# Spectral block with a Mish MLP: order of the normalisation, banks of the first two items, place of the last deviations, order of the last contraction

## The chip, the cores and the metric

The kernel runs on one core of a Trainium2 chip. The metric is the device time of one execution in microseconds (us). A core has five engines with queues of their own, each of which works through its instructions in order: TensorE (PE in the profile; its weight loads are PEld), VectorE (DVE), ScalarE (ACT), GpSimd (POOL) and SyncE (SP), which here issues the transfers. They wait for one another through semaphores. Matmuls write into PSUM, of which the kernel uses eight banks of 128 x 512 fp32 numbers; ScalarE and VectorE read them, GpSimd does not.

## What is computed

One block with two residual branches over x (1 x 2048 x 512, fp32). Six modulation vectors come from c.

```python
mod = (_silu(c) @ w_mod).reshape(c.shape[0], 6, 1, -1)
sa, ca, ga, sb, cb, gb = (mod[:, i] for i in range(6))
h = _layernorm(x, axis=-1) * (1 + ca) + sa
x = x + ga * irfft2(rfft2(h) * (w_r + 1j * w_i))
h = _layernorm(x, axis=-1) * (1 + cb) + sb
h = einsum("bsd,df->bsf", h, w1) + b1
act = h * tanh(softplus(h))
x = x + gb * einsum("bsf,fd->bsd", act, w2)
```

The change touches the second branch (the layer norm, the MLP with Mish, 512 -> 1376 -> 512) and its borders.

## The kernel before

The 2048 rows are held as 16 tiles x[:, n, :] of 128 rows. The first branch is a DFT written as matmuls, in three phases. Its last phase runs over the 16 tiles: p3_col(n) multiplies into a bank "A" and ScalarE copies it out, p3_row(n) multiplies into a bank "B" and VectorE adds it to x[:, n, :] (line 650). norm_sums(n) (lines 109 to 112) then takes the mean and variance of the row on VectorE, and norm_scale(lo, hi) (lines 126 to 130) turns the variances of a few tiles into reciprocal deviations: Ln and Exp on ScalarE (norm_guess, lines 116 and 117), then four small operations on VectorE. Between these steps the loop at line 870 prepares w1 and the first w2 pieces: load_w2 is a transfer, gate_w2 multiplies by gb on GpSimd, sum_w2 makes four differences in tsum on GpSimd, split_w2 casts on ScalarE and subtracts on VectorE. All large products are done in fp32r with a high part and a low part (three products).

The second branch goes through 8 blocks of two row tiles (256 rows). Each block has 6 items t = 0 to 5 of the hidden layer: t = 0 is the piece of 96 columns left over, the others are two pieces of 128. So there are 48 items, numbered g = 6 b + t. For an item:

- up(g), line 719: 12 or 24 matmuls of w1 with the normalised block, into one of two banks "A". It needs an empty bank.
- mish(g), line 729: ScalarE's Mish out of that bank (line 735; this empties the bank), four additions and subtractions on VectorE (line 748) that build the seven operands of a seven-product scheme, and casts to the high part `ah` on ScalarE (line 754). `ah` has two buffers, so the cast waits until down(g - 2) has read the old one.
- low(parts), line 758: the low part `al` on VectorE (line 760).
- down(g), line 762: 21 matmuls (6 for t = 0) into the six banks of the block, two "C", two "B", two "D". It runs two items behind up (LAG = 2). RAW and SUM (lines 24 and 25) give the order of the seven groups of three matmuls: the first of RAW goes to bank 0, the next two to the halves of banks 1 and 2, then SUM to banks 3, 4, 5 and the other half of bank 1.

After the last down of a block, in item t = 1 of the next, gather copies banks 0, 4, 5 and 3 out into two buffers `h` on ScalarE (line 790), residual adds banks 2 and 1 to the two rows on VectorE (line 801), and spread does the remaining additions on GpSimd (chain, lines 795 and 796, and the four functions of rows_of, lines 807 to 810). Then store issues two transfers.

The next block's input is made in between. norm_pair(n) (line 606) normalises two tiles on ScalarE (line 140, one activation for each), into the same two buffers `h`; transpose_in (line 609) turns half of them by four matmuls (line 616) into a bank "A"; split_in (line 619) scales, shifts and splits them on ScalarE and VectorE (lines 624 to 629). norm_pair is issued in item t = 3, the transposes ahead of up in t = 4 and t = 5.

The order within each engine is the order in which the program issues its instructions (manual_schedule): mlp(s), lines 826 to 844, is one item, and the lines 899 to 924 lead from the spectral branch into the items and to finish (line 846), which does the last block's sums, on VectorE but for the function `own`, and stores its rows one after the other.

Of the kernel before, what the change touches and what calls it, by code (L numbers as in the profile page):

```python
# [15 lines left out]
N2 = 16  # L16
# [3 lines left out]
NT = 6  # L20
# [2 lines left out]
TERMS = ((0, 0), (0, 1), (1, 0))  # L23
RAW = ((0, None, 0, 0), (1, 0, 2, 1), (2, 0, 1, 6))
SUM = ((3, None, 3, 3), (4, None, 4, 4), (5, None, 5, 5), (1, 1, 6, 2))
LAG = 2


@with_exitstack
def tile_spectral_block(ctx: ExitStack, tc: tile.TileContext, x_d, w1_d, b1_d, w2_d,  # L30
                        c_d, xt_d, wm_d, wq_d, wz_d, kr_d, km_d, kc_d, ki_d, kf_d, kv_d, kw_d, kp_d, out_d):
    nc = tc.nc
# [16 lines left out]
    def bank(tag):  # L49
        return psum.tile([P, 512], F32, name="bank", tag=tag)  # L50

    def buf(tag, dt=F32):
        return work.tile([P, 512], dt, name="buf", tag=tag)
# [60 lines left out]
    def norm_guess(lo, hi):  # L114
        r = rstd[:, lo:hi]
        nc.scalar.activation(r, mv[:, lo:hi, 1], AF.Ln, bias=eps)
        nc.scalar.activation(r, r, AF.Exp, scale=-0.5)

    def norm_refine(lo, hi, sign):
        r = rstd[:, lo:hi]  # L120
        t = small.tile([P, 4], F32, name="ve")[:, 0:hi - lo]
        for out, a, one, op in ((t, mv[:, lo:hi, 1], EPS, ALU.add), (t, t, -0.5 * sign, ALU.mult),
                                (r, t, 1.5 * sign, ALU.add)):
            nc.vector.scalar_tensor_tensor(out, a, one, r, op0=op, op1=ALU.mult)  # L124

    def norm_scale(lo, hi):
        norm_guess(lo, hi)
        norm_refine(lo, hi, 1)
        nc.vector.scalar_tensor_tensor(nmr[:, lo:hi], mv[:, lo:hi, 0], -1.0, rstd[:, lo:hi],
                                       op0=ALU.mult, op1=ALU.mult)  # L130
# [6 lines left out]
    def norm(n, late=False):  # L137
        h = buf("h")
        if late:
            nc.scalar.activation(h, x[:, n, :], AF.Identity, scale=rstd[:, n:n + 1], bias=nmr[:, n:n + 1])  # L140
            return h
        nc.gpsimd.tensor_scalar(h, x[:, n, :], rstd[:, n:n + 1], nmr[:, n:n + 1],
                                op0=ALU.mult, op1=ALU.add)
        return h
# [461 lines left out]
    def norm_pair(n):  # L606
        st["h2", n] = norm(n, True), norm(n + 1, True)
# [84 lines left out]
    def split_w2(t, sums):  # L692
        hi, lo = w2[t]
        if t == 0:
            split(hi[:96], lo[:96], st.pop(("w2", 0))[0])
            return
        h, l = (w.rearrange("p e d -> p (e d)") for w in (hi, lo))
        if sums:
            split(h[:, 768:], l[:, 768:], tsum.rearrange("p e d -> p (e d)"))
        else:  # L700
            u, v = st["w2", t]
            split(h[:, 0:256], l[:, 0:256], u[:, 0:256])
            split(h[:, 256:768], l[:, 256:768], v)
# [12 lines left out]
    ups, acts, out_ps, done = {}, {}, {}, {}  # L716
    tsum = modr[:, 0:2].rearrange("p r (e d) -> p (r e) d", d=256)

    def up(g):
        b, t = divmod(g, NT)  # L720
        ups[g] = ps = bank("A")
        hh, hl = h2[b]
        parts = [(w, h, k) for w, h in ((w1h, hh), (w1l, hh), (w1h, hl)) for k in range(4)]
        for e, f, rows in tiles(t):
            for i, (w, h, k) in enumerate(parts):
                nc.tensor.matmul(ps[:rows, 256 * e:256 * e + 256], w[:, k, f * P:f * P + rows], h[:, k, :],  # L726
                                 start=(i == 0), stop=(i == 11))

    def mish(g):
        b, t = divmod(g, NT)  # L730
        ps = ups.pop(g)
        w = buf("g1")
        for e, f, rows in reversed(tiles(t)):
            c = slice(256 * e, 256 * e + 256)
            nc.scalar.activation(w[:rows, c], ps[:rows, c], AF.Mish, bias=b1n[:rows, f:f + 1])  # L735
        hi, lo = (act.tile([P, 7, P], F32R, name=n) for n in ("ah", "al"))
        acts[g] = hi, lo
        if t == 0:
            parts = [(w[:rows, 0:256], slice(0, 2))]
        elif g == total - 1:  # L740
            parts = [(w, slice(0, 4))]
        else:
            u = buf("g2")
            a = w.rearrange("p (e s) -> p e s", s=P)
            v = u.rearrange("p (e s) -> p e s", s=P)
            for o, p, q, op in ((v[:, 0], a[:, 0], a[:, 2], ALU.add), (v[:, 1], v[:, 0], a[:, 1], ALU.subtract),
                                (v[:, 2], a[:, 1], a[:, 0], ALU.subtract), (v[:, 3], a[:, 3], v[:, 1], ALU.subtract)):
                nc.vector.tensor_tensor(o, p, q, op=op)  # L748
            parts = [(w[:, P:], slice(0, 3)), (u, slice(3, 7))]
        flat = []  # L750
        for r, c in parts:
            n = r.shape[0]
            h, l = (z[:n, c].rearrange("p e s -> p (e s)") for z in (hi, lo))
            nc.scalar.copy(h, r)  # L754
            flat.append((l, r, plain(h)))
        return flat

    def low(parts):
        for l, r, h in parts:
            nc.vector.tensor_tensor(l, r, h, op=ALU.subtract)  # L760

    def down(g):
        b, t = divmod(g, NT)
        a = acts.pop(g)
        if t == 0:
            out_ps[b] = out = [bank(n) for n in "CBBCDD"]
            for n, half in ((1, 1), (2, 0)):
                for i, (p, q) in enumerate(TERMS):
                    nc.tensor.matmul(out[n], a[p][:96, half], w2[0][q][:96], start=(i == 0), stop=False)  # L769
            return  # L770
        out = out_ps[b]
        if g == total - 1:
            for n, half in ((2, 0), (1, 1)):
                for f in range(2):
                    for i, (p, q) in enumerate(TERMS):
                        nc.tensor.matmul(out[n], a[p][:, half + 2 * f], w2["plain"][q][:, 512 * f:512 * f + 512],
                                         start=False, stop=(f == 1 and i == 2))
            return
        for n, half, e, r in RAW + SUM:
            o = out[n][:, 0:256] if half is None else out[n][:, 256 * half:256 * half + 256]  # L780
            last = t == 5 or (half is None and g == total - 2)
            for i, (p, q) in enumerate(TERMS):
                nc.tensor.matmul(o, a[p][:, e], w2[t][q][:, r], start=(half is None and t == 1 and i == 0),  # L783
                                 stop=(last and i == 2 and (n, half) != (1, 0)))
# [38 lines left out]
    total = NB * NT  # L823
    ctx.enter_context(tc.manual_schedule())

    def mlp(s):
        b, t = divmod(s, NT)
        nxt = 2 * b + 2 if b < NB - 1 else None
        if t in (4, 5) and nxt:
            transpose_in(nxt, t - 4)  # L830
        up(s)
        if t in (4, 5) and nxt:
            split_in(nxt, t - 4)
        parts = mish(s)
        if t == 3 and nxt:
            norm_pair(nxt)
        down(s - LAG)
        if t == 1 and b:
            gather(b - 1)
            residual(b - 1)  # L840
        low(parts)
        if t == 1 and b:
            spread(b - 1)
            store(b - 1)

    def finish():
        b = NB - 1
        down(total - 2)
        gather(b)
        own, ahead, far, both = rows_of(b)  # L850
        chain(b, nc.vector)
        far(nc.vector)
        own(nc.gpsimd)
        both(nc.vector)
        down(total - 1)
        residual(b, (0,))
        store(b, (0,))
        ahead(nc.vector)
        residual(b, (1,))
        store(b, (1,))  # L860

    apply_gate()
    prep = {s: [] for s in range(N2 + 1)}
    for t, s in ((1, 1), (2, 6), (3, 11)):
        for lag, fn, *args in ((-1, load_w2, t), (0, gate_w2, t, 0), (1, gate_w2, t, 1), (2, split_w2, t, False),
                               (2, sum_w2, t, 0, 1), (3, sum_w2, t, 2, 3), (5, split_w2, t, True)):
            prep[s + lag].append((fn, args))
    prep[14].append((load_w2, (0,)))
    prep[15].append((gate_w2, (0, 0)))
    for s in range(N2 + 1):  # L870
# [25 lines left out]
            norm_pair(0)  # L896
        if s in (7, 8):
            split_in(0, s - 7)
    norm_scale(N2 - 4, N2)
    split_w2(0, False)  # L900
    parts = mish(0)
    low(parts)
    parts = mish(1)
    low(parts)
    load_w2(4)
    gate_w2(4, 0, 1)
    sum_w2(4, 0, 1, 2, 3)
    for s in range(LAG, total):
        mlp(s)
        if s == 3:  # L910
            split_w2(4, False)
            split_w2(4, True)
            load_w2(5)
            gate_w2(5, 0, 1)
            sum_w2(5, 0, 1, 2, 3)
        if s == 5:
            split_w2(5, False)
            split_w2(5, True)
        if s == total - 5:
            load_w2(5)  # L920
            gate_w2(5, 0, 1)
        if s == total - 3:
            plain_w2()
    finish()


# [134 lines left out]
```

## Time and profile before

| | |
|---|---|
| median of 3 runs | 440.3 us (438.82 to 440.44) |
| the profiled execution, device time | 439.86 us |
| its span, first to last instruction | 438.0 us |
| granted TensorE clock, mean | 0.97 |
| time from first MLP matmul (up(0)) to the end of the span | 156.3 to 438.0 us |
| ACT_TABLE_LOAD instructions | 2 (one at the start, one ahead of the first Mish) |

A line of the page's groups or of the timeline names the source line, the engine, the operation, what it writes and reads, and the count. In the timeline the first two numbers are start and length in us, and the brackets at the end give the idle time of the engine before it and what ended that. The chain of waits is followed back from the last instruction: at each step the work that released the next. "PEclk" is the clock that TensorE was granted, as a share of full speed. TensorE's matmuls are pipelined, so a group of them is shorter than the sum of their single lengths.

### The profile page before, as it was taken

Reading aid. Unit: us, or ns where it says so; the run is one execution under the profiler, and the core shown is the slowest. Engines: PE = TensorE matmul, PEld = TensorE weight load, DVE = VectorE, ACT = ScalarE, POOL = GpSimd, SP = SyncE. Lnnn points to the kernel's source line nnn. Section 1 sums busy time; section 2 is a strip of 40 time slices with the busy share of each in tenths; the row PEclk is TensorE's granted clock in tenths of the full one; section 3 lists DMA queues with packets and bytes.
Section 4 is the critical chain, followed back from the end, with each engine's and each line's share of the span. In section 5 each row is a group of like instructions: output and inputs, shape, how many; then the busy total and the mean of one; then the engine's idle time right before and its main releaser. Section 6 shows DMA issues by size and latency. Waiting matters only on the chain.

```text
span 438.0 us, 8143 instructions
## 1 busy us (share of the span) xinstructions
PE 404.8 (92%) x3152; PEld 389.9 (89%) x3152; DVE 279.2 (64%) x541; ACT 217.2 (50%) x496; POOL 152.5 (35%) x181
## 2 busy tenths in 40 slices
PE   8999899999999879899899899899899899989995
PEld 8888689899999878799799799799799799889994
DVE  2999958774299996686554644643743843833854
ACT  2777646677357345553444443533543532542441
POOL 0677536563268764324102201400500500500521
PEclk9999999999999998899899899899999989989999
DMA  8999843462024311100100100100100100100021
GB/s 281 362 345 351 249 167 99 135 248 71 28 64 130 114 43 26 48 2 3 47 1 1 48 1 1 49 1 1 49 1 0 49 1 0 50 0 1 30 69 48
DMA packets 20903, 35.25 MB, mean 80 GB/s; under 512 B 3713, under 2 KB 6561, under 8 KB 20481
## 3 DMA queue, kind: packets, MB, share of 16 engines
q1 hardware_dynamic: 20432, 34.21, 23.3%
q8 instruction: 25, 0.41, 0.4%
q10 hardware_dynamic: 432, 0.53, 0.3%
q14 instruction: 14, 0.11, 0.1%
HBM read 30.53 MB, written 4.19 MB: 79 GB/s over the span
## 4 chain that ended last, share of the span: by engine, by line
PE 69%; DVE 19%; ACT 7%; issue 2%; DMA 1%; POOL 1%; SPq 0%; ACTq 0%; DVEq 0%; POOLq 0%
PE bank L726 30%; PE bank L783 22%; DVE st L111 4%; PE bank L455 3%; PE bank L501 3%; PE bank L769 3%; DVE ve L124 2%; ACT buf L140 2%; PE bank L616 2%; DVE x L650 2%; ACT ah L754 2%; PE bank L488 2%; DMA x<-in_A_x_dram 1%; PE bank L434 1%; DVE buf L226 1%
## 5 line engine op out<-in xcount | busy, mean ns | idle before, releaser
L748 DVE TENSOR_TENSOR buf<-buf 128x128 f32<-128x128 f32 x156 | 54.5, 390 | 53.3 <-ACT buf L735 51.8
L760 DVE TENSOR_TENSOR al<-buf,ah 128x512 fp32r<-128x512 f32 (+2 forms) x87 | 64.0, 759 | 38.1 <-ACT ah L754 38.1
L754 ACT CAST ah<-buf 128x512 fp32r<-128x512 f32 (+2 forms) x87 | 45.3, 552 | 80.5 <-PE bank L783 48.5
L795 POOL TENSOR_TENSOR buf<-buf 128x256 f32<-128x256 f32 x7 | 5.2, 739 | 182.7 <-ACT buf L790 182.7
L735 ACT ACTIVATE buf<-bank,b1n 128x256 f32<-128x256 f32 (+1 forms) x88 | 37.3, 470 | 57.8 <-PE bank L726 57.8
L726 PE MATMUL bank<-h,w1h 128*128 128x256 f32 (+1 forms) x352 | 57.5, 298 | 2.8 <-ACT buf L735 2.8
L726 PE MATMUL bank<-h2o,w1h 128*128 128x256 f32 (+1 forms) x352 | 56.3, 294 | 0.0
L726 PEld LDWEIGHTS bank<-h,w1h 128*128 128x128 f32 (+1 forms) x352 | 50.3, 202 | 3.3 <-ACT buf L735 3.0
L726 PEld LDWEIGHTS bank<-h2o,w1h 128*128 128x128 f32 (+1 forms) x352 | 49.5, 198 | 0.3
L783 PE MATMUL bank<-w2a,ah 128*128 128x256 f32 x168 | 36.3, 283 | 0.0
L783 PE MATMUL bank<-w2b,ah 128*128 128x256 f32 x161 | 34.4, 283 | 0.0
L726 PE MATMUL bank<-h,w1l 128*128 128x256 f32 (+1 forms) x176 | 30.1, 297 | 0.0
L726 PE MATMUL bank<-h2o,w1l 128*128 128x256 f32 (+1 forms) x176 | 29.3, 291 | 0.0
L783 PEld LDWEIGHTS bank<-w2a,ah 128*128 128x128 f32 x168 | 28.1, 191 | 0.0
L783 PEld LDWEIGHTS bank<-w2b,ah 128*128 128x128 f32 x161 | 26.9, 192 | 0.0
L616 PE MATMUL bank<-ident,buf 128*128 128x128 f32 x64 | 12.7, 307 | 15.1 <-ACT buf L140 15.1
L679 POOL TENSOR_TENSOR buf<-buf,modr 128x512 f32<-128x512 f32 (+1 forms) x13 | 17.2, 1329 | 26.2 <-DMA buf<-in_B_w_dram 14.3
L726 PEld LDWEIGHTS bank<-h,w1l 128*128 128x128 f32 (+1 forms) x176 | 25.8, 202 | 0.0
L233 PE MATMUL bank<-buf,mring 128*128 128x512 f32 x48 | 21.4, 446 | 4.2 <-DVE buf L226 1.9
L637 PE MATMUL bank<-kc,d 128*128 128x128 f32 x128 | 24.8, 276 | 0.5 <-ACT d L359 0.5
L726 PEld LDWEIGHTS bank<-h2o,w1l 128*128 128x128 f32 (+1 forms) x176 | 25.2, 197 | 0.0
L111 DVE BATCH_NORM_STATS2 st<-x 128x6 f32<-128x512 f32 x32 | 22.0, 687 | 4.4 <-DMA x<-in_A_x_dram 3.9
(200 smaller groups left out, 1014.0 us busy)
## 6 DMA issues: line engine op xcount, KB each, us to landing
buf<-in_B_w_dram SPq DMA_DIRECT2D x20, 256.0 KB, 2.7
xring<-in_x_t_dram SPq DMA_DIRECT2D x16, 256.0 KB, 4.6
x<-in_A_x_dram SPq DMA_DIRECT2D x16, 256.0 KB, 5.1
wm<-in_w_mod_dram SPq DMA_DIRECT2D x16, 256.0 KB, 4.4
out_dram<-x SPq DMA_DIRECT2D x16, 256.0 KB, 2.0
mraw<-in_km_dram SPq DMA_DIRECT2D x16, 128.0 KB, 4.6
wqa<-in_w_q_dram SPq DMA_DIRECT2D x8, 256.0 KB, 4.2
wqb<-in_w_q_dram SPq DMA_DIRECT2D x8, 256.0 KB, 4.8
```

What stands on the lines that cost most here:

```text
L111: nc.vector.bn_stats(t, x[:, n, :])
L233: nc.tensor.matmul(pa, m[:, a, 0:128], g, start=(i == 0), stop=False)
L455: nc.tensor.matmul(pb[:, 0:w].rearrange("p (e q) -> p e q", q=nq)[:, :, i], z[:, i * P:(i + 1) * P], kf[:, 0:128], start=True, stop=True)
L616: nc.tensor.transpose(ps[:, (2 * k + i) * P:(2 * k + i + 1) * P], h[:, (2 * g + k) * P:(2 * g + k + 1) * P], ident)
L637: nc.tensor.matmul(o, dj[:, 0:128], kc[0][:, n, :], start=True, stop=False)
L679: nc.gpsimd.tensor_tensor(r, r, gbr[:r.shape[0]], op=ALU.mult)
L726: nc.tensor.matmul(ps[:rows, 256 * e:256 * e + 256], w[:, k, f * P:f * P + rows], h[:, k, :], start=(i == 0), stop=(i == 11))
L735: nc.scalar.activation(w[:rows, c], ps[:rows, c], AF.Mish, bias=b1n[:rows, f:f + 1])
L748: nc.vector.tensor_tensor(o, p, q, op=op)
L754: nc.scalar.copy(h, r)
L760: nc.vector.tensor_tensor(l, r, h, op=ALU.subtract)
L783: nc.tensor.matmul(o, a[p][:, e], w2[t][q][:, r], start=(half is None and t == 1 and i == 0), stop=(last and i == 2 and (n, half) != (1, 0)))
```

## The change

Five things are altered.

- mlp: norm_pair of the next block is issued ahead of mish(s) in item t = 3, no longer behind it.
- up: items 0 and 1 write into banks "C" instead of "A". (The first block's down takes the "C" banks later.)
- The start of the items: mish(0) comes first, ahead of split_w2(0) and of the second split of w2[3], which is left out of the preparation loop and issued behind mish(1).
- norm_scale of the last four tiles (their reciprocal deviations) is issued after item 2 * NT + 2 = 14, in the third block, instead of ahead of mish(0). The tiles are needed from item 33 on.
- The end: down(46) (total - 2) goes through its seven groups in the order END, in which the four banks that gather copies are finished first, and finish runs `own` on VectorE instead of GpSimd.

```diff
--- before.py
+++ after.py
@@ -23,6 +23,7 @@
 TERMS = ((0, 0), (0, 1), (1, 0))
 RAW = ((0, None, 0, 0), (1, 0, 2, 1), (2, 0, 1, 6))
 SUM = ((3, None, 3, 3), (4, None, 4, 4), (5, None, 5, 5), (1, 1, 6, 2))
+END = (RAW[0], SUM[1], SUM[2], SUM[0], RAW[1], RAW[2], SUM[3])
 LAG = 2
 
 
@@ -718,7 +719,7 @@
 
     def up(g):
         b, t = divmod(g, NT)
-        ups[g] = ps = bank("A")
+        ups[g] = ps = bank("C" if g < 2 else "A")
         hh, hl = h2[b]
         parts = [(w, h, k) for w, h in ((w1h, hh), (w1l, hh), (w1h, hl)) for k in range(4)]
         for e, f, rows in tiles(t):
@@ -776,7 +777,7 @@
                         nc.tensor.matmul(out[n], a[p][:, half + 2 * f], w2["plain"][q][:, 512 * f:512 * f + 512],
                                          start=False, stop=(f == 1 and i == 2))
             return
-        for n, half, e, r in RAW + SUM:
+        for n, half, e, r in END if g == total - 2 else RAW + SUM:
             o = out[n][:, 0:256] if half is None else out[n][:, 256 * half:256 * half + 256]
             last = t == 5 or (half is None and g == total - 2)
             for i, (p, q) in enumerate(TERMS):
@@ -831,9 +832,9 @@
         up(s)
         if t in (4, 5) and nxt:
             split_in(nxt, t - 4)
-        parts = mish(s)
         if t == 3 and nxt:
             norm_pair(nxt)
+        parts = mish(s)
         down(s - LAG)
         if t == 1 and b:
             gather(b - 1)
@@ -850,7 +851,7 @@
         own, ahead, far, both = rows_of(b)
         chain(b, nc.vector)
         far(nc.vector)
-        own(nc.gpsimd)
+        own(nc.vector)
         both(nc.vector)
         down(total - 1)
         residual(b, (0,))
@@ -864,7 +865,8 @@
     for t, s in ((1, 1), (2, 6), (3, 11)):
         for lag, fn, *args in ((-1, load_w2, t), (0, gate_w2, t, 0), (1, gate_w2, t, 1), (2, split_w2, t, False),
                                (2, sum_w2, t, 0, 1), (3, sum_w2, t, 2, 3), (5, split_w2, t, True)):
-            prep[s + lag].append((fn, args))
+            if s + lag < N2:
+                prep[s + lag].append((fn, args))
     prep[14].append((load_w2, (0,)))
     prep[15].append((gate_w2, (0, 0)))
     for s in range(N2 + 1):
@@ -896,12 +898,10 @@
             norm_pair(0)
         if s in (7, 8):
             split_in(0, s - 7)
-    norm_scale(N2 - 4, N2)
+    low(mish(0))
     split_w2(0, False)
-    parts = mish(0)
-    low(parts)
-    parts = mish(1)
-    low(parts)
+    low(mish(1))
+    split_w2(3, True)
     load_w2(4)
     gate_w2(4, 0, 1)
     sum_w2(4, 0, 1, 2, 3)
@@ -916,6 +916,8 @@
         if s == 5:
             split_w2(5, False)
             split_w2(5, True)
+        if s == 2 * NT + 2:
+            norm_scale(N2 - 4, N2)
         if s == total - 5:
             load_w2(5)
             gate_w2(5, 0, 1)
```

## Prediction

> **What bounds the kernel now.** I read the page first, then who waited for whom on TensorE, then the chain of waits, then a table of stretches. A row is start, length, engine, line, operation.
>
> ```profile
> PE 404.8 (92%) x3152; PEld 389.9 (89%) x3152; DVE 279.2 (64%) x541; ACT 217.2 (50%) x496; POOL 152.5 (35%) x181
> ```
>
> ```profile
> PE bank L616 <- ACT buf L140: 15.1, 14, 1.8
> PE bank L726 <- ACT buf L735: 2.8, 1, 2.8
> ```
>
> TensorE (PE) bounds the program, and only two waits of size interrupt it in the second half: 14 waits of the transposes (line 616) on the normalisation (line 140), two in each of the seven changes of block, and one of up(2) on mish(0). The chain shows one change of block (the second), and the one after it where the transposes do not wait:
>
> ```profile
> 211.11 1.03 ACT ah L754 x2
> 212.14 1.43 ACT buf L140 x2
> ...
> 213.62 0.57 PE bank L616 x3
> 214.19 4.34 PE bank L726 x24
> ...
> 221.05 0.44 PE bank L616 x4
> 221.48 2.84 PE bank L726 x24
> ```
>
> Item t=3 of a block has its casts (line 754) wait until down of t=1 has read the old `ah`. The normalisation of the next block stands behind those casts in ScalarE's queue, so it begins when TensorE has nothing left to do. Then the 24 matmuls of up take 4.34 us, where they take 2.84 us elsewhere. The table of stretches, each from the end of that down to the end of the next up, shows why; its columns are the stretch, its length, busy time (count) of PE, PEld, DVE, ACT and POOL, then PEclk, the granted clock:
>
> ```profile
> 176.47:183.95 7.48, 5.33 (x31) 5.04 (x31) 4.59 (x7) 5.13 (x9) 1.43 (x1) 0.77 0.24 70
> 211.03:218.53 7.50, 5.35 (x31) 5.06 (x31) 2.65 (x6) 3.48 (x6) 0.00 (x0) 0.77 0.00 0
> 245.61:253.10 7.49, 5.34 (x31) 5.05 (x31) 2.69 (x6) 3.47 (x6) 0.00 (x0) 0.77 0.00 0
> 280.18:287.47 7.29, 5.14 (x31) 4.84 (x31) 2.70 (x6) 3.48 (x6) 0.00 (x0) 0.77 0.00 1
> 314.55:320.52 5.97, 3.82 (x31) 3.52 (x31) 2.69 (x6) 3.48 (x6) 0.00 (x0) 1.00 0.00 0
> 347.60:355.10 7.50, 5.35 (x31) 5.05 (x31) 2.69 (x6) 3.48 (x6) 0.00 (x0) 0.77 0.00 0
> 382.18:389.64 7.46, 5.31 (x31) 5.01 (x31) 2.70 (x6) 3.48 (x6) 0.00 (x0) 0.77 0.00 1
> 162.43:165.21 2.78, 0.01 (x1) 0.01 (x1) 2.34 (x6) 2.69 (x6) 0.10 (x1) 1.00 0.00 0
> 165.21:169.84 4.63, 4.63 (x25) 4.63 (x26) 3.38 (x7) 2.24 (x5) 2.11 (x2) 0.63 0.24 60
> ```
>
> In six of the seven changes, and after up(2)'s wait, the clock falls after the idle time. A stall costs its own 2.2 us and some 1.5 us of slow matmuls after it. Without stall and slow clock such a stretch would be 0.44 + 2.84 = 3.28 us.
>
> **Normalisation ahead of the fourth item.** Nothing is added; two activations of line 140 change places with mish's. What they need is: ScalarE free of mish of t=2, and the two `h` buffers, which the POOL adds of the previous block's result hold. The fourth change of block shows when that is (timeline, up(15) and what surrounds it):
>
> ```profile
> 277.16 1.44 POOL L810 TENSOR_TENSOR x<-x,buf 128x512 f32<-128x512 f32 x1
> 277.47 0.63 ACT L754 CAST ah<-buf 128x512 fp32r<-128x512 f32 x1 [2.16 <-DVE buf L748]
> 278.00 0.83 ACT L735 ACTIVATE buf<-bank,b1n 128x256 f32<-128x256 f32 x2
> 280.26 1.03 ACT L754 CAST ah<-buf 128x384 fp32r<-128x384 f32 x2 [1.43 <-PE bank L783]
> 281.20 1.51 ACT L140 ACTIVATE buf<-x,nmr,rstd 128x512 f32<-128x512 f32 x2
> ```
>
> ScalarE is free at 278.00. The first norm would run from there for about 0.72 us, the second from 278.72, after POOL gave its buffer back at 278.60 (margin 0.12 us). Both are done at 278.00 + 1.43 = 279.43, ahead of TensorE's 280.18, so the transposes do not wait. Behind them in the queue mish(15) ends at 279.43 + 0.83 = 280.26 instead of 278.83. Who waits for it: up(16), which reuses the bank A that mish(15) empties, from 280.18 + 0.44 = 280.62 on (margin 0.36 us). VectorE's subtractions of item 15 and its casts come later too, but down reads them two items on. If the cover is gone, each microsecond of delay past 0.36 is one of TensorE's idle time. The other changes with POOL adds have the same order; the first has none. So six stretches (all but the fourth, which is treated next) come to 3.28 us: 7.48 + 7.50 + 7.49 + 5.97 + 7.50 + 7.46 = 43.40, less 6 x 3.28 = 19.68, gives **23.7 us**.
>
> **The last deviations in the third block.** norm_scale(12..16) leaves the start of the MLP and is issued after item 14, just ahead of the fourth change of block. It brings Ln and Exp between two Mish. Their rows, at the place that they leave:
>
> ```profile
> 157.30 0.63 PE L726 MATMUL bank<-h,w1h 128*96 128x256 f32 x4
> 158.34 1.05 ACT L689 CAST w2hi<-modr 128x1024 fp32r<-128x1024 f32 x1 [2.10 <-POOL modr L686]
> 159.81 2.72 POOL L679 TENSOR_TENSOR buf<-buf,modr 96x512 f32<-96x512 f32 x2 [1.50 <-DMA buf<-in_B_w_dram]
> 162.11 0.18 DVE L112 BATCH_NORM_AGGREGATE mv<-st 128x2 f32<-128x6 f32 x1
> 162.33 0.30 ACT L116 ACTIVATE rstd<-mv,eps 128x4 f32<-128x4 f32 x1 [2.94 <-DVE mv L112]
> 162.66 0.20 ACT L117 ACTIVATE rstd<-rstd 128x4 f32<-128x4 f32 x1
> 162.77 0.60 ACT L689 CAST w2b<-buf 96x512 fp32r<-96x512 f32 x1
> 163.39 1.28 ACT L735 ACT_TABLE_LOAD   x1
> 164.68 0.47 ACT L735 ACTIVATE buf<-bank,b1n 96x256 f32<-96x256 f32 x1
> ```
>
> One table load served the way from Ln and Exp to Mish; the new place needs one back and one forth. ScalarE, from 278.00: load 1.28, Ln 0.33 (to Exp's start), Exp 0.20, both norms 1.43, load 1.28, mish 0.83, which ends at 283.35. The second norm ends at 281.24; the transposes wait for it, then up(16) waits for the bank until 283.4: some 2.8 us of idle time, no shorter than now. With a slow clock (4.3 us, as in the chain) up(16) would end at 287.7, against 287.47: a **loss of 0.2 us**, which I take, since six of seven stalls of some 2.2 us brought a slow clock; with a full clock (2.84) it ends at 286.2, a gain of 1.3. Should Ln and Exp need a load each, 1.28 more: loss 1.5. VectorE's four small refinements lie in its gap before mish(15). This change of block thus keeps its stall.
>
> The row of the load shows 1.28 us, and the Mish starts 0.01 us behind its end. Against this step stands a rule of the Trainium skill (ScalarE: Activation LUTs, "Rules for kernel authors"): activations are to be grouped by table set, and each switch to another set is to be reckoned at about 2.7 us, the load and a drain. By that page, two switches would take some 2.8 us more than by the row, and the sum below would end at 413.8 as an estimate.
>
> **First two items.** What leaves ScalarE's queue ahead of mish(0) is the cast at 158.34 and Ln and Exp, which waited until 162.3 for VectorE's last statistics. up(0) is done at 157.93; ScalarE was idle before 158.34 and again for 2.94 us. So the table load and mish(0) (0.47) and its cast end before 159. VectorE makes mish(0)'s low part after its statistics, from 162.3 to 162.7 and the low part of w2[0] (its gate is done on POOL in the first half of the pair at 159.81, at about 161.2; a cast of 0.6 follows) until 163.4; down(0) needs both only at 165.3. mish(1) follows up(1), which ends at 162.43. The banks C let up(2) and up(3) take the two banks A, which ScalarE's last cast of the spectral stage left before it went idle, 2.10 us ahead of 158.34; up(2) starts at 162.43 instead of 165.21 and goes at full clock: 2.78 + 4.63 - 2.84 = **4.6 us**. The moved split of w2[3] (its cast is the 1.05 us at 158.34) lands on ScalarE behind mish(1)'s casts, at about 165, and on VectorE behind its subtractions; mish(2) behind it is ready at about 167, and up(3), in the other bank, does not need it. Bounds: the clock stays slow (3.1), or nothing of it is lost (4.6).
>
> **Tail.** down(46) fills the four banks that gather reads in its first 12 matmuls instead of all 21, and `own` goes from POOL to VectorE.
>
> ```profile
> 427.52 0.62 ACT L754 CAST ah<-buf 128x512 fp32r<-128x512 f32 x1 [1.61 <-PE bank L783]
> ...
> 429.39 1.01 ACT L790 COPY buf<-bank 128x256 f32<-128x256 f32 x3 [0.97 <-PE bank L783]
> ...
> 430.67 1.51 DVE L809 TENSOR_TENSOR x<-x,buf 128x256 f32<-128x256 f32 x1
> ...
> 432.21 0.69 DVE L810 TENSOR_TENSOR x<-x,buf 128x512 f32<-128x512 f32 x1
> ...
> 432.43 0.39 PE L776 MATMUL bank<-w,al 128*128 128x512 f32 x1
> 433.01 0.69 DVE L801 TENSOR_TENSOR x<-x,bank 128x512 f32<-128x512 f32 x1
> 433.62 0.42 DVE L808 TENSOR_TENSOR x<-x,buf 128x256 f32<-128x256 f32 x1
> ...
> 434.14 0.69 DVE L801 TENSOR_TENSOR x<-x,bank 128x512 f32<-128x512 f32 x1
> ```
>
> The copies follow the cast from 428.14 at about 0.34 us each, and end at 429.5, not 430.4. VectorE's chain is done at about 429.8; then `far` takes 0.42 (as line 808, with POOL silent, not 1.51), `own` 0.69 and `both` 0.69 (as line 810): 431.6. Row 0 is added by 432.3, `ahead` by 432.8, and row 1 waits for TensorE's last matmul (432.82) and ends at 433.6 instead of 434.83: **1.2 us**. TensorE now ends last. If VectorE is still slow, 0.5 at least.
>
> **Sum** against the profiled span of 438.0: 438.0 - 23.7 + 0.2 - 4.6 - 1.2 = 408.7 us. The profiled execution took 439.86, 1.86 more than its span; the median, 440.3, is 0.44 above it. So 408.7 + 1.86 + 0.44 = **411.0 us**, a ratio of 0.933.
>
> **Rivals.**
>
> The wait moves behind the transposes (chance 0.15). The margins of 0.12 us at POOL and 0.36 us at the bank are thin. If POOL's adds, or VectorE's 2.2 us hold on the cast at 277.47, end about 1 us later against TensorE, up waits 0.6 to 1.0 us in the five changes of block with POOL adds: 414 to 416, 415 in the middle. Against it: those adds begin with gather, at t=1, and everything between is paced by TensorE without a stall, so the distances should stay.
>
> The switch of tables costs more than the load (0.10). If ScalarE first had to empty itself, as long again as the load, it is 2 x 1.28 = 2.6 us more at the fourth change: 413.6. For it: ScalarE is busy up to the new place, as it was before the old load. Against it: the load started 0.02 us behind the end of the cast at 162.77, and the Mish 0.01 us behind the load. The Trainium skill (ScalarE: Activation LUTs, "What ACT_TABLE_LOAD costs") has such a drain.
>
> The slow clock is not from the idle time but from the transposes or the change of weights (0.05). Then the five stretches that had it and up(2) keep about 1.5 us each: 6 x 1.5 = 9, 420. Against it: the second pair of transposes (221.05) is followed by 2.84 us.
>
> ScalarE's queue is blocked (0.04), the side on which it is slower. The second norm waits for its `h` buffer, and in front of it no mish can pass; up waits for the bank. The price in each of five changes is the delay less 0.36 us, and the slow clock's 1.5 us again. To eat the 29.3 us of the forecast it takes 29.3 / 5 - 1.5 + 0.36 = 4.7 us of delay: POOL's last add would have to end past 283 instead of at 278.6. At 6 us it is 5 x 7.14 = 35.7 more than the forecast, 446.7. Only a spread that starts an item later could do it, and nothing in its issue order changes.
>
> **How the numbers follow.** The forecast has 0.66, with its own range 408.5 (full clock at the fourth change, and the runs' scatter of some 0.8) to 413. The range over the cases is 407.5 to 418: it leaves out the slow-clock case, the blocked queue, and a little on both sides. A difference under 0.5% (2.2 us) is what a measurement of this kernel can hardly tell from none. All cases but the blocked queue are far beyond it: faster 0.95, same 0.01, slower 0.04.
>
> **What would show it.** Right: line 616's wait falls from 15.1 us to two waits in the fourth change; PEclk 1.00 in the other changes of block; the stretch from the end of down to the end of up at 3.3 us instead of 6.0 to 7.5; three loads of tables in all beside the preload; up(2) without a wait; line 809 at 0.42 us. Wrong: up waiting for line 735 in every block (bank A), a slow clock without idle time, or more loads.

## The result, and the profile after

| | before | changed |
|---|---|---|
| median | 439.56 us (4 runs) | 416.05 us (4 runs, 414.8 to 416.27) |
| ratio, 95% interval | | 0.9465 (0.9425 to 0.9506) |
| profiled execution: span | 438.0 us | 414.2 us |
| granted clock, mean | 0.97 | 0.989 |

The kernel is faster by 5.4%; 411.0 us and a ratio of 0.933 were forecast, so the sum was 5 us short. The changed file has one line more near its top, so a line of before stands one number higher (726 is 727, 735 is 736). First, who waited for whom on TensorE (total, times, longest):

```profile
PE bank L617 <- ACT buf L141: 2.3, 3, 1.7
...
PE bank L727 <- ACT buf L736: 1.8, 2, 1.6
...
PE bank L727 <- DVE h2o L629: 0.8, 1, 0.8
```

The 15.1 us of the transposes on the normalisation are 2.3, and what is left sits in a few places. Three stretches, each from the end of down(t = 1) to the end of up(t = 4), show them: the first change of block, the second, and the third (columns as before).

```profile
172.24:176.41 4.17, 3.77 (x31) 3.30 (x29) 3.25 (x9) 3.59 (x8) 0.00 (x0) 1.00 0.01 2
204.78:208.06 3.28, 3.28 (x30) 3.28 (x29) 2.76 (x8) 2.03 (x4) 0.00 (x0) 1.00 0.00 0
235.26:245.17 9.91, 6.26 (x30) 5.83 (x31) 3.92 (x12) 6.48 (x11) 0.00 (x0) 0.66 0.00 0
```

The second is the 3.28 us of the forecast, with the clock at 1.00; the fourth to seventh take 3.27 or 3.28 us, with the same clock. The third, where the last deviations now stand, has become longer than before (7.49). ScalarE's timeline there:

```profile
232.43 0.62 ACT L755 CAST ah<-buf 128x512 fp32r<-128x512 f32 x1 [2.16 <-DVE buf L749]
233.07 1.28 ACT L117 ACT_TABLE_LOAD   x1
234.36 0.30 ACT L117 ACTIVATE rstd<-mv,eps 128x4 f32<-128x4 f32 x1
234.68 1.28 ACT L118 ACT_TABLE_LOAD   x1
235.97 0.20 ACT L118 ACTIVATE rstd<-rstd 128x4 f32<-128x4 f32 x1
236.08 1.50 ACT L141 ACTIVATE buf<-x,nmr,rstd 128x512 f32<-128x512 f32 x2
237.60 1.28 ACT L736 ACT_TABLE_LOAD   x1
238.90 0.84 ACT L736 ACTIVATE buf<-bank,b1n 128x256 f32<-128x256 f32 x2
```

There are three loads here, not two: Ln and Exp each have one, since nothing names the set that holds both, as the start of the kernel does. TensorE, with nothing to do from 235.25, sees this (idle time and its cause in brackets), and the first matmuls after it are slow, 1.22 us for four where 0.64 is usual:

```profile
236.94 0.33 PE L617 MATMUL bank<-ident,buf 128*128 128x128 f32 x1 [1.69 <-ACT buf L141]
237.64 0.55 PE L617 MATMUL bank<-ident,buf 128*128 128x128 f32 x3 [0.38 <-ACT buf L141]
239.79 1.22 PE L727 MATMUL bank<-h,w1h 128*128 128x256 f32 x4 [1.60 <-ACT buf L736]
```

The starts of up give the whole account: the distance between two of them before and after, taken from the first matmul of each. The forecast's term stands beside it.

| stretch | before | changed | difference | forecast |
|---|---|---|---|---|
| start of the program to up(1) | 159.34 | 159.74 | +0.40 | 0 |
| up(1) to up(3) | 11.70 | 7.14 | -4.56 | -4.6 |
| first change, up(3) to up(5) | 15.61 | 12.40 | -3.21 | -4.2 |
| up(6) to up(7) | 3.94 | 4.95 | +1.01 | 0 |
| second change, up(9) to up(11) | 15.62 | 11.50 | -4.12 | -4.2 |
| third change, up(15) to up(17) | 15.61 | 18.14 | +2.53 | -4.2 |
| fourth change, up(21) to up(23) | 15.40 | 11.50 | -3.90 | +0.2 |
| fifth to seventh change | 45.29 | 34.51 | -10.78 | -11.1 |
| up(47) to the end of the span | 16.00 | 14.78 | -1.22 | -1.2 |

All other distances are equal to 0.01 us. The sum is -23.85, which is 438.03 - 414.19. (The forecast had the deviations at the fourth change; they stand at the third, as told below.)

The end, TensorE's last group and VectorE:

```profile
405.43 1.35 ACT L791 COPY buf<-bank 128x256 f32<-128x256 f32 x4
...
407.03 0.42 DVE L810 TENSOR_TENSOR x<-x,buf 128x256 f32<-128x256 f32 x1
...
409.36 0.61 PE L777 MATMUL bank<-w,ah 128*128 128x512 f32 x2
...
410.24 0.69 DVE L802 TENSOR_TENSOR x<-x,bank 128x512 f32<-128x512 f32 x1 [0.33 <-PE bank L777]
```

The copies run without a gap behind the cast, `far` (line 810) takes 0.42 us, not 1.51, and the last addition now waits for TensorE.

### The profile page after: what moved, and what is told of

Its sections match the earlier page's. It is cut to its first block, busy times and chain, and to the rows that moved or that the text cites. A ratio compares the mean times of both kernels' runs of the same rounds, so it can differ in the third digit from the quotient of the medians.

```text
span 414.2 us, 8147 instructions
## 1 busy us (share of the span) xinstructions
PE 394.8 (95%) x3152; PEld 381.5 (92%) x3152; DVE 281.2 (68%) x542; ACT 220.8 (53%) x499; POOL 152.0 (37%) x180
## 4 chain that ended last, share of the span: by engine, by line
PE 65%; DVE 23%; ACT 6%; issue 2%; DMA 2%; POOL 1%; SPq 0%; DVEq 0%; POOLq 0%; ACTq 0%
PE bank L727 26%; PE bank L784 21%; DVE st L112 4%; PE bank L456 3%; PE bank L502 3%; DVE ve L125 3%; DVE buf L749 2%; PE bank L770 2%; DVE x L651 2%; PE bank L489 2%; DMA x<-in_A_x_dram 2%; PE bank L435 1%; DVE w2a L691 1%; DVE buf L227 1%; DVE buf L207 1%
## 5 line engine op out<-in xcount | busy, mean ns | idle before, releaser
L749 DVE TENSOR_TENSOR buf<-buf 128x128 f32<-128x128 f32 x156 | 56.8, 405 | 44.4 <-ACT buf L736 43.0
L727 PE MATMUL bank<-h,w1h 128*128 128x256 f32 (+1 forms) x352 | 55.0, 290 | 1.8 <-ACT buf L736 1.8
L727 PE MATMUL bank<-h2o,w1h 128*128 128x256 f32 (+1 forms) x352 | 53.5, 283 | 0.8 <-DVE h2o L629 0.8
L727 PEld LDWEIGHTS bank<-h,w1h 128*128 128x128 f32 (+1 forms) x352 | 47.9, 193 | 2.6 <-ACT buf L736 2.2
L727 PEld LDWEIGHTS bank<-h2o,w1h 128*128 128x128 f32 (+1 forms) x352 | 46.4, 186 | 1.3 <-DVE h2o L629 1.0
L727 PE MATMUL bank<-h,w1l 128*128 128x256 f32 (+1 forms) x176 | 28.8, 288 | 0.0
L727 PE MATMUL bank<-h2o,w1l 128*128 128x256 f32 (+1 forms) x176 | 28.0, 282 | 0.0
L638 PE MATMUL bank<-kc,d 128*128 128x128 f32 x128 | 24.8, 276 | 0.5 <-ACT d L360 0.5
L639 PE MATMUL bank<-kc,d 128*128 128x128 f32 x128 | 24.7, 275 | 0.0
L727 PEld LDWEIGHTS bank<-h,w1l 128*128 128x128 f32 (+1 forms) x176 | 24.6, 193 | 0.0
L727 PEld LDWEIGHTS bank<-h2o,w1l 128*128 128x128 f32 (+1 forms) x176 | 23.8, 186 | 0.0
```

The lines of the kernel that those rows point to most:

```text
L638: nc.tensor.matmul(o, dj[:, 0:128], kc[0][:, n, :], start=True, stop=False)
L639: nc.tensor.matmul(o, dj[:, 64:192], kc[1][:, n, :], start=False, stop=True)
```

## The experiments

The start of the items differs by up to 3 us between executions (up(0) at 155.5 to 158.8; the reason was not traced), so where a few microseconds count I give the time from the start of up(0) to the end of the span: 281.8 us in the kernel before, 257.6 in the changed one.

**The normalisation put back behind mish**, all else changed:

```diff
-        if t == 3 and nxt:
-            norm_pair(nxt)
         parts = mish(s)
+        if t == 3 and nxt:
+            norm_pair(nxt)
```

> The changed kernel, with the next block's normalisation issued behind mish of item t = 3 again; all else stays changed. Theory (this one move carries nearly the whole gain, and ScalarE's place ahead of the casts is what counts): six changes of block lose what they gained (about 22 us by the starts of up), and in the third the normalisation comes behind mish as well as behind the table loads (about 2 us more), less the 1 us wait of up(6), which goes: span about 437, within 2 of the kernel before. Rival (the gain comes from several parts, the early start, the banks and the tail with it): the span rises by less than 18, to 432 or below.

Measured: span 438.8, median 438.87, ratio to the kernel before 0.9982 (0.9955 to 1.0008); 283.2 us from up(0). The whole gain is gone, with the early start and the tail still in the kernel: what these bring, 5.8 us, goes in the third change (20.5 us from up(15) to up(17), 15.6 before), in the first (16.6 us, 15.6 before) and in the fifth. The transposes' wait is back:

```profile
PE bank L617 <- ACT buf L141: 19.7, 14, 5.6
```

In this execution the fifth change, which had kept its full clock in the kernel before, went slow with the same stall (15.6 us from up(27) to up(29) against 14.1). The clock thus does not fall with certainty after such a stall.

**The two lines alone, in the kernel before.**

```diff
-        parts = mish(s)
         if t == 3 and nxt:
             norm_pair(nxt)
+        parts = mish(s)
```

> The kernel before, with only the two lines of the normalisation exchanged. Theory (the stall and the slow clock behind it vanish in all seven changes of block, the third too, since no table loads stand there): 438.0 less about 27 is a span of 410 to 412, below the 414.2 of the changed kernel, though the early start and the tail (4.6 and 1.2) are not in it. Rival (the moved deviations or the banks are needed for the move to work): 414 or more.

Measured: span 411.4, median 413.44, ratio 0.9418 (0.9385 to 0.945); 253.4 us from up(0), 4.2 less than the changed kernel. No wait of the transposes is left, in any change, and all seven take 11.5 us from up(t = 3) to up(t = 5). One exchange of two lines is as good as or better than the whole change.

**The last deviations back at their old place**, ahead of mish(0).

```diff
+    norm_scale(N2 - 4, N2)
     low(mish(0))
...
-        if s == 2 * NT + 2:
-            norm_scale(N2 - 4, N2)
```

> The changed kernel, with the last deviations taken back to their old place, ahead of mish(0). One table load in all beside the first. Theory (the loads cost the third change of block 6.6 us; in front of mish(0) they hold up down(0) and the first normalisation by about 3): the third change takes 3.3 us instead of 9.9, span 410 to 411.5. Rival (the deviations were put away from the start for good reason, and ahead of mish(0) they cost what they did before, 4.6): 412 or more.

Measured: span 411.9, median 412.57, ratio 0.9393 (0.9352 to 0.9435). The third change is at 11.5 us from up(15) to up(17), 6.6 less. The start gives back 3.06: up(2) to up(3) 5.38 instead of 4.22, up(3) to up(4) 8.48 instead of 6.58. Both sizes are as the theory had them; the span is 0.4 past its upper end and 0.1 short of the rival's 412, with up(0) 1.2 us later. Of the rival's 4.6 us the start costs 3.1.

**The last deviations after item 17.**

```diff
-        if s == 2 * NT + 2:
+        if s == 2 * NT + 5:
```

> The changed kernel, with the last deviations issued after item 17 (t = 5) instead of item 14 (t = 2). The three table loads stay. Theory (what the loads cost depends on who waits behind them: mish(18) is needed only two items on, and its bank later still): third change 3.3 us, up(18) to up(20) without a wait, span 407.6. Rival (three loads of 1.28 us and the emptying of ScalarE cost the same wherever they stand): 413 or more.

Measured: span 406.1, median 408.38, ratio 0.9304 (0.9271 to 0.9338). ScalarE's timeline there:

```profile
246.38 1.28 ACT L117 ACT_TABLE_LOAD   x1
247.67 0.30 ACT L117 ACTIVATE rstd<-mv,eps 128x4 f32<-128x4 f32 x1
247.99 1.28 ACT L118 ACT_TABLE_LOAD   x1
249.28 0.21 ACT L118 ACTIVATE rstd<-rstd 128x4 f32<-128x4 f32 x1
249.51 1.28 ACT L736 ACT_TABLE_LOAD   x1
250.80 0.47 ACT L736 ACTIVATE buf<-bank,b1n 96x256 f32<-96x256 f32 x1
251.31 0.41 ACT L755 CAST ah<-buf 96x256 fp32r<-96x256 f32 x1
252.17 0.84 ACT L736 ACTIVATE buf<-bank,b1n 128x256 f32<-128x256 f32 x2 [0.46 <-DVE al L761]
```

The same three loads cost TensorE nothing here: no distance between two ups changes after it (up(17) to up(21) as in the kernel before), and by up(19) ScalarE has caught up and waits again. What a load costs is decided by who is queued behind it.

**Ln and Exp in one set**, still after item 14.

```diff
         if s == 2 * NT + 2:
+            nc.scalar.preload_act_table_set("natural_log_exp_and_others")
             norm_scale(N2 - 4, N2)
```

> The changed kernel, with the table set that holds both Ln and Exp loaded by name ahead of the last deviations, so that two loads stand in the third change of block instead of three. Theory (the price of that change is the loads one by one, 1.28 us each, and the slow clock behind the idle time): idle time 1.28 us shorter, the clock still low; the change takes 8.2 to 8.6 us instead of 9.9, span 412.5 to 413. Rival (a switch costs about twice the load): a load taken away gives 2.6 us or more, span 411.6 or less.

Measured: span 411.1, median 413.07, ratio 0.9411 (0.9366 to 0.9456); 253.9 us from up(0), 3.7 less than the changed kernel. The span is below the theory's 412.5 to 413 and looks like the rival, but the rows say otherwise:

```profile
233.47 1.28 ACT L920 ACT_TABLE_LOAD   x1
234.77 0.30 ACT L117 ACTIVATE rstd<-mv,eps 128x4 f32<-128x4 f32 x1
235.10 0.21 ACT L118 ACTIVATE rstd<-rstd 128x4 f32<-128x4 f32 x1
...
236.73 1.28 ACT L736 ACT_TABLE_LOAD   x1
238.03 0.84 ACT L736 ACTIVATE buf<-bank,b1n 128x256 f32<-128x256 f32 x2
```

```profile
236.06 0.33 PE L617 MATMUL bank<-ident,buf 128*128 128x128 f32 x1 [0.41 <-ACT buf L141]
236.77 0.55 PE L617 MATMUL bank<-ident,buf 128*128 128x128 f32 x3 [0.38 <-ACT buf L141]
238.92 0.74 PE L727 MATMUL bank<-h,w1h 128*128 128x256 f32 x4 [1.60 <-ACT buf L736]
...
241.39 0.64 PE L727 MATMUL bank<-h,w1h 128*128 128x256 f32 x4
```

TensorE's first wait is 0.41 us instead of 1.69: the load taken away is worth 1.28 us and no more (up(16) comes 8.78 us behind up(15), not 10.06). The rest, 2.3 us from up(16) to up(17), is the clock, which stayed full where the theory had it low: 5.82 us instead of 8.08. The waits here, 0.41, 0.38 and 1.60, add up to more than the 1.78 and 0.38 that brought a slow clock in six changes of the kernel before; so the idle time alone does not settle when the clock falls, and no run here shows what does.

**Items 0 and 1 in the banks A again.**

```diff
-        ups[g] = ps = bank("C" if g < 2 else "A")
+        ups[g] = ps = bank("A")
```

> The changed kernel, with items 0 and 1 in the banks A again. Theory (mish(0) is now early enough, done at 160.1, and mish(1) at 163.7, while up(2) asks for its bank at 162.7 and up(3) at 165.5; so the banks C bring nothing beside the early mish): up(2) starts as it does, span 414.2, no change. Rival (the banks C are what lets up(2) start, as the prediction had it): up(2) waits 2.8 us, with a slow clock behind it, span about 418.8.

Measured: span 414.8, median 415.23, ratio 0.9465 (0.9431 to 0.9498); 256.8 us from up(0), and up(1), up(2) and up(3) are 2.92 and 4.22 us apart, as in the changed kernel. The banks bring nothing beside the early mish. (The 0.8 us less from up(0) are in the third change, 17.34 us from up(15) to up(17) instead of 18.14: the same stall, with a granted clock of 0.81 instead of 0.66 behind it.)

**The banks alone, in the kernel before.**

```diff
-        ups[g] = ps = bank("A")
+        ups[g] = ps = bank("C" if g < 2 else "A")
```

> The kernel before, with only items 0 and 1 in the banks C. Read from the starts of up(1), up(2) and up(3): 5.9 and 5.8 us apart in the kernel before, 2.9 and 4.2 in the changed one. Theory (banks C and an early mish(0) each take up(2)'s wait away; with the banks alone down(0) then waits for the late mish(0) instead): 2.9 and about 5.2. Rival (the banks bring nothing by themselves): 5.9 and 5.8. The other changes of block keep their stall, and the span is near 434 to 435.

Measured: 2.92 and 4.22 us, not 5.2: up(2)'s wait is gone with the banks alone too, and down(0) does not wait; in this execution mish(0), 4.6 us after the start of up(1) (5.3 before), came just in time (its low part was done at 166.99, and down(0) asked for it at 167.29). By these rows it would have been some 0.5 us late with the 5.3 us of the kernel before, so the missing wait is shown for this execution alone. Part of the gain is lost soon after: the transposes of the first change wait longer (longest 3.8 us, 1.8 before), and from up(3) to up(5) it is 17.3 us instead of 15.6. From up(0) to the end it is 276.5 us, 5.2 less than the kernel before (span 435.3, a single execution), but only 2.9 of this is left of up(1) to up(5); 1.6 is the clock, which stayed full in the second and sixth change (14.1 us each) and fell in the fifth.

**The tail put back.**

```diff
-        for n, half, e, r in END if g == total - 2 else RAW + SUM:
+        for n, half, e, r in RAW + SUM:
...
-        own(nc.vector)
+        own(nc.gpsimd)
```

> The changed kernel, with the old order of down(46) and with own on GpSimd. Read from the trace: from the first matmul of down(46) to the end of the span it is 9.4 us in the changed kernel. Theory (VectorE's chain ends last again): 10.6 us, as in the kernel before. Rival (TensorE ends last either way): 9.4 to 9.6.

Measured: from the start of up(47) to the end of the span 16.02 us, against 14.78; the kernel before has 16.00. So the end is 1.2 us longer, as the theory had it (a single execution). The 1.2 us are the tail's two edits; their shares were not tried.

**GpSimd's work on w2[4] and w2[5] left out.**

```diff
     load_w2(4)
-    gate_w2(4, 0, 1)
-    sum_w2(4, 0, 1, 2, 3)
...
             load_w2(5)
-            gate_w2(5, 0, 1)
-            sum_w2(5, 0, 1, 2, 3)
```

> The changed kernel, with GpSimd's gate and differences of the w2 pieces 4 and 5 left out (those pieces are not multiplied by gb, and their sums are stale). Theory (VectorE's steps of items 2 and 4 take 3.1 and 3.7 us instead of 1.0 because GpSimd works on these pieces at the same time, and this delays the first normalisation by 0.9 us and up(6) by 1.0): VectorE takes about 1.0 us for them, the first change 3.3 us instead of 4.2, no wait at up(6), span 412.3. Rival (VectorE or ScalarE is late for its own order, the w2 splits behind item 3): the waits stay, 414.2.

Measured: span 411.4, median 413.13, ratio 0.9407 (0.9369 to 0.9445). VectorE's four steps of item 2, in the changed kernel and then without GpSimd's work:

```profile
167.53 3.07 DVE L749 TENSOR_TENSOR buf<-buf 128x128 f32<-128x128 f32 x4
```

```profile
167.19 1.02 DVE L749 TENSOR_TENSOR buf<-buf 128x128 f32<-128x128 f32 x4
```

up(3) to up(4) is 5.72 us instead of 6.58, and up(6) to up(7) 3.94 instead of 4.95: without GpSimd's work neither wait that the forecast had not seen is left. The Trainium skill (GPSIMD Engine Reference, "Specifications") says that GpSimd's SBUF interfaces are shared with VectorE, with contention where VectorE's instructions read two SBUF inputs, as these do; the trace agrees, with a factor of 3.

For the first change this is only part of the account. VectorE's four steps of item t = 2 are as long in every later block, 2.95 to 2.98 us beside GpSimd's adds in the changed kernel, and no transpose waits there but in the third change, behind the loads. What sets the first block apart is when they start: 0.66 us behind the first matmul of up(3), and in the later blocks 0.31 us ahead of that of up(t = 3). First the rows of the changed kernel that stand ahead of its 3.07 us, then the same steps in the fourth block of the kernel before (up(21) starts at 274.77):

```profile
165.32 1.04 ACT L690 CAST w2hi<-modr 128x1024 fp32r<-128x1024 f32 x1
166.27 0.83 ACT L736 ACTIVATE buf<-bank,b1n 128x256 f32<-128x256 f32 x2
166.39 1.23 DVE L691 TENSOR_TENSOR w2a<-modr,w2hi 128x1024 fp32r<-128x1024 f32 x1 [0.26 <-ACT w2hi L690]
```

```profile
274.47 2.97 DVE L748 TENSOR_TENSOR buf<-buf 128x128 f32<-128x128 f32 x4 [0.80 <-ACT buf L735]
```

The cast and the subtraction are the split of w2[3] that the change itself moved there. Mish(2) begins 3.61 us after the start of up(2) instead of 3.05 as in a later block, and VectorE then needs 0.43 us more to come to its steps instead of 0.03: together about 1 us, by which they start late. No run has the split at another place with GpSimd's work kept, so this share is read from the rows and not shown by an experiment.

**The first normalisation earlier**, from the kernel with the deviations after item 17.

```diff
     low(mish(0))
+    norm_pair(2)
     split_w2(0, False)
...
-        if t == 3 and nxt:
+        if t == 3 and nxt and b:
```

> The kernel of e4_dev_late, with the first of these normalisations (tiles 2 and 3) issued behind mish(0) instead of in item 3, where ScalarE's last cast of item 2 waits for a VectorE slowed by GpSimd. Theory (ScalarE is idle there for 1.6 us in all, the h buffers are free, and mish(3) then follows the cast at once): from the start of up(3) to that of up(4) 5.7 us instead of 6.6, mish(1) not later, from the start of up(0) to the end of the span 249.4 to 249.8 instead of 250.6. Rival (mish(0)'s successors are pushed back and down(0) or up(3) waits): 250.6 or more.

Measured: up(3) to up(4) 5.71 us, as expected; but up(6) to up(7) is 5.10 instead of 4.56. From up(0) to the end it is 250.3 us against 250.6, short of the 249.4 to 249.8 of the theory, median 408.36 against 408.38, ratio 0.9314 (0.9284 to 0.9344). TensorE comes to up(6) earlier, and VectorE's half of the next block's input, behind GpSimd's work on w2[5], does not: most of the gain is given back. (How much is uncertain: up(6) to up(7) is 4.56 to 4.95 us in four executions whose kernels are the same up to there.) This and the kernel with the deviations after item 17 are the best of the study, 7% faster than the kernel before.

## Why the prediction was right, and where its sum was short

The measured 416.05 us lies in the range over all cases, 407.5 to 418, and outside the forecast's own range, 408.5 to 413. It is next to the 414 to 416 of the first rival, by chance: that rival had a wait in five changes of block, and none of the five has it.

- *Six changes of block at 3.28 us, 23.7 us.* Right in mechanism: in the changed kernel, where the normalisation is ahead of mish and no table load stands ahead of it, neither a long stall nor a slow clock is left. Undone, it takes everything with it; alone, it gives 0.9418. Five changes (the second and the fourth to seventh) came within about 0.1 us of the term each. The first kept 1.0 us, and two steps failed there. "The other changes with POOL adds have the same order; the first has none" overlooked GpSimd's work on w2[4], though the table of stretches has GpSimd busy just ahead of that change (2.11 us from 165.21 to 169.84). And the moved split of w2[3] was held against up(3) alone ("does not need it"), not against the normalisation, which stands behind item 2's last cast: VectorE's four steps start about 1 us late behind that split, and last 3.07 us. This is the shape of the first rival, VectorE's hold on the cast ending about 1 us later, in a change that the rival left out.
- *The margins of 0.12 and 0.36 us in the other changes.* They held: no wait appears in the second and the fourth to seventh.
- *A loss of 0.2 us from the last deviations.* Item 14 is ahead of the third change, not the fourth; the rows quoted for its sum are of items 20 to 22, one block later, where the distances are nearly the same (15.4 us and 15.6), so only the label was wrong. The size was wrong: +2.5 us. Of the 2.3 that were missed, 1.28 is the third load ("one load back and one forth"; the bound with a load each was named and not taken). The rest is up(16), 5.38 us (239.79 to 245.17 in the chain of waits) instead of 4.3. Some 0.2 of it is the measure: the 4.34 and 2.84 us of the chain begin behind the last transpose, which the first matmuls overlap, while up from a standing start takes 3.1 us at full clock (238.92 to 242.03 with one set). The other 0.8 is a clock lower than assumed, and this much is one execution's: with the banks A again and with the tail put back, the same stall gives 17.34 and 17.39 us from up(15) to up(17), not 18.14. The prediction had named "more loads" than three beside the preload as a sign of being wrong; there are four.
- *The rival that a switch costs twice the load*, and with it the 2.7 us of the Trainium skill (ScalarE: Activation LUTs, "Rules for kernel authors"): fell. Each load is 1.28 us, the next activation begins 0.01 us behind it, and a load less is worth 1.28 us. That loads between activations of different sets are dear was right only in the place where the normalisation is queued behind them.
- *Start, 4.6 us.* Right in size (4.56), wrong in its cause: "the banks C let up(2) and up(3) take the two banks A". The early mish frees the old banks in time by itself, and up(2) does not wait with the banks by themselves either (one execution). The two edits are not a sum, they are alternatives at this point, and with the banks alone, the normalisation still behind mish, part of the gain was lost again in the first change.
- *up(6)*, 1.0 us, was in no term: with the start and the first change both shorter, TensorE reaches up(6) before a VectorE slowed by GpSimd's work on w2[5] has the input ready. With the two lines alone, where up(3) comes later, up(6) to up(7) is 4.11 us, 0.17 over the kernel before.
- *Tail, 1.2 us.* Right, and for the reason given.
- *The blocked queue and the slow clock without idle time.* Neither appeared: the six changes without the loads keep a clock of 1.00, transposes and change of weights included.

## What to carry to other kernels

In an in-order queue, put work that waits for nothing ahead of work whose wait is long: two exchanged lines were worth 6%, because the wait of a cast was handed on to everything behind it, and to TensorE's clock. Once such a stall is gone, ask which helpers it had covered, since they become late next (here the preparation of w2 in the first block, on GpSimd beside VectorE and in the queues of ScalarE and VectorE). Look at where a table load stands and not only at how many there are: three of them cost 5.8 to 6.6 us, with the slow clock, ahead of a normalisation that TensorE waits for, and nothing three items later.

## What was not expected of the hardware

TensorE's granted clock did not follow the idle time alone. The same stall, 1.78 us and 0.33 to 0.38, stands in 18 changes of block: seven of the kernel before (six went slow), five of the kernel with the normalisation put back (all five) and six of the kernel with the banks alone (four; the second and the sixth kept 1.00). The clock also fell after 1.69, 0.38 and 1.60 us in the changed kernel, but not after 0.41, 0.38 and 1.60 with one set, nor after 1.54, 0.38 and 0.17 with the last deviations back. Its price is up to 2.3 us for 24 matmuls (5.38 against 3.11 us from the start of the first to the end of the last). What decides it stays open.
